# The first weight piece's products token tile by token tile, two norms on ScalarE, and weights rounded in units of two pieces

## The chip, the cores and the metric

The kernel runs on one core of one Trainium2 chip. The metric is the device time of one execution in microseconds; the time of a kernel is the median of its runs. Before the change it is 1092.45 us, the median of 9 runs from 1089.96 to 1096.31. A profiled execution gives the start and duration of every instruction on each engine: TensorE (PE in the profile; its weight loads PEld), VectorE (DVE), ScalarE (ACT), GpSimd (POOL) and the queue of SyncE that issues transfers (SPq).

## The reference

`x` comes from an attention in chunks of 64 tokens (8 batches, 8 heads, 576 tokens, head size 64), with heads side by side, so that it is 8 x 576 x 512. Then:

```python
X = np.fft.fft(x, axis=1)
X = np.fft.fft(X, axis=2)
u = x + np.real(X).astype(np.float32)
mu = np.mean(u, axis=-1, keepdims=True)
var = np.mean((u - mu) ** 2, axis=-1, keepdims=True)
un = (u - mu) / np.sqrt(var + 1e-06)
out = u + np.maximum(un @ w_ch1, 0.0) @ w_ch2      # w_ch1 512 x 2048, w_ch2 2048 x 512
```

The weights are given in double precision; the kernel computes in 32 bits, so it has to round each weight itself.

## The kernel before

**Tokens.** Tokens are taken in tiles of 128. Four tiles of a batch (two "low" and two "high", mirrored ones) make a group; each pair of batches also has a tile of the remaining tokens. Group 0 is batch 0.

**Start.** `attention_early` computes batch 0's attention. `fourier_early` then multiplies by the tables of the transform along the tokens into four sums `z` and a row `mid` (L742, L745), copies them to `zf` and `zr` (L752 to L768), and multiplies by the tables along the features into `early_xp` (L772). For each pair of tiles it adds the result to `x` (L786 to L790), takes mean and variance (`means`, L634 to L639: two instructions on VectorE, then logarithm and exponential on ScalarE), norms the tile (`normed`, L820 to L826), and transposes it on TensorE into `unT` (`turned`, copies on L839). Where TensorE would wait, `keep_warm` gives it products of zeros (L1143).

**The two layers.** `up_first` takes group 0 through the first layer: for each four of the sixteen feature tiles it goes over four weight pieces (kk), with four products of 512 token columns for each, and then ScalarE takes the relus (L940). `down_plain` goes over the sixteen pieces of the second layer (`dn`, L970), four products each. Each such group of four products is one step of the main loop, which counts them in `t`: steps 1 to 16 end in `up_first`, step 17 and on in `down_plain`. After every step the loop draws from a list of side work (attention and Fourier of the next batch, `side`), and then rounds weights: one call of `round_next`, two calls in steps up to 4, at every fourth and from step 19, and none where the side work says it was heavy. Batch 1's side work falls in steps 3 to 25; its last softmax of a tile comes at step 14, folds at 16 and 18, its sums `z` at 22 and 23, its mixes at 24 and 25. From step 23, `conv2` (L897) adds work on VectorE. Group 1's tiles are normed and turned from the tenth piece of `dn` on. Every engine carries out its instructions in the order in which the program names them.

**Rounding.** A weight piece is 128 x 512 doubles, read as pairs of 32-bit words, `lo` and `hi`. There are 32 pieces, 16 for each layer. `round_weight(i)` issues what this text calls the head of piece i and then the tail of piece i - 1. A head is two ANDs on VectorE (L306, L309), each followed by ScalarE: `fraction` (L300), and `exponent` with two instructions (L303, L304). A tail is three instructions on VectorE (L318 to L320), after which the piece can be used. Raw pieces lie in seven spaces, five later on; a piece is loaded (L285, on SP's queue) when a tail has freed a space. The first heads and the first tail are issued at the end of `attention_early`; the ScalarE part of piece 1 is put off until after the first copies of `fourier_early`.

**PSUM.** `ps_f` has four buffers of a bank each (`idle`, `early_xp`, `mid`, later `up` and `dn`), `ps_a` one of two banks (scores, half of `z`), `ps_t` two for transposes and mixes.

Of the kernel before, what the change touches and what calls it, by code (L numbers as in the profile page):

```python
# [16 lines left out]
def kernel(  # L17
# [32 lines left out]
    nc = tc.nc  # L50
# [66 lines left out]
    for b in range(B):  # L117
# [20 lines left out]
    spaces = [yall.rearrange("p a b -> p (a b)")[:, i * 1024:(i + 1) * 1024] for i in range(2)] + [  # L138
        xall[:, r:r + 2, :].rearrange("p a f -> p (a f)")[:, 0:1024]
        for r in (2 * G, 2 * G + 2, NR + 1, G, G + 2)  # L140
    ]
    N_LATE, N_EARLY, N_LAST = 5, 8, 26
# [129 lines left out]
    power = {}  # L272

    raws, free = {}, list(range(len(spaces)))

    def raw(i):
        return spaces[raws[i]].bitcast(U32).rearrange("p (f r) -> p f r", r=2)

    def load_weight(i):

        fit = [r for r in free if (i < N_EARLY or r < N_LATE) and (i < N_LAST or r > 1)]
        if i < len(pieces) and fit:
            raws[i] = fit[0]
            free.remove(fit[0])
            nc.sync.dma_start(out=raw(i).rearrange("p f r -> p (f r)"), in_=pieces[i][1].bitcast(U32))  # L285

    def round_weight(i, later=None):
# [6 lines left out]
        if i < len(pieces):  # L294
            w, t = pieces[i][0], raw(i)
            lo, hi, wi = t[:, :, 0], t[:, :, 1], w.bitcast(U32)
            p = power[i] = three_p.tile([128, 512], U32, tag="o", name="power")
# [4 lines left out]
            def exponent(p=p):  # L302
                nc.scalar.activation(out=p, in_=p, func=ACTF.Relu, scale=-1.0, bias=top[:, 0:1])  # L303
                nc.scalar.activation(out=p, in_=p, func=ACTF.Relu, scale=-8.0, bias=top[:, 1:2])  # L304
# [5 lines left out]
            if later is None:  # L310
                exponent()
            else:
                later += [fraction, exponent]
        if 0 < i <= len(pieces):
            w, t = pieces[i - 1][0], raw(i - 1)
            lo, hi = t[:, :, 0], t[:, :, 1]
            p = power.pop(i - 1)
# [3 lines left out]
            r = raws.pop(i - 1)  # L321
            if i - 1 + len(spaces) < N_EARLY or r < N_LATE:
                free.append(r)
            load_weight(max(raws, default=i - 1) + 1)
# [203 lines left out]
    def attention_early():  # L528
# [32 lines left out]
        keep_warm(6)  # L561
        turn_tables()
        round_next()
        round_next(put_off)

    def attention(b):

# [706 lines left out]
```

## Time and profile before

| | us |
|---|---|
| median of 9 runs | 1092.45 |
| lowest, highest | 1089.96, 1096.31 |
| the profiled execution | 1090.56 |
| its span, first to last instruction | 1088.8 |
| TensorE busy | 1072.3 |
| VectorE busy | 577.2 |
| ScalarE busy | 298.2 |
| GpSimd busy | 280.9 |
| first product of `up_first` | 52.93 |
| first product of `dn` | 121.76 |
| first transposes of group 1 | 174.31 |

A line of the timeline gives the start in us, the time until the last of the merged instructions ends, the engine, the line of the kernel, the operation, what it writes and reads, partitions x elements, how many instructions are merged, and in brackets how long the engine sat idle before and what released it. Durations overlap at their ends, since the next instruction starts before the last has written all it has; so the distance between two starts is what an instruction costs its engine. The granted clock of TensorE is 1.00 in all slices, 0.999 in the mean.

### The profile page before, as it was taken

What the parts mean: (1) busy time and instruction counts of PE and PEld (TensorE: products, weight loads), DVE (VectorE), ACT (ScalarE), POOL (GpSimd) and SP (SyncE); (2) the same over time, 40 slices, a digit from 0 to 9 for tenths busy, and PEclk for the clock granted to TensorE, in tenths of its full rate; (3) what the DMA queues carried; (4) which work ended last, traced back from release to release, by engine and by line L of the source; (5) the groups of instructions that cost most, each with busy time, mean ns of one, the idle gap of its engine ahead of it and who ended that gap; (6) DMA issues with size and microseconds to landing.
All of it is one profiled execution on the core that took longest, in us unless ns stands there. A gap on an engine that the chain in (4) does not pass through costs nothing.

```text
span 1088.8 us, 18830 instructions
## 1 busy us (share of the span) xinstructions
PE 1072.3 (98%) x7016; PEld 849.5 (78%) x7016; DVE 577.2 (53%) x1260; ACT 298.2 (27%) x725; POOL 280.9 (26%) x403
## 2 busy tenths in 40 slices
PE   8999999999999999999999999999999999999998
PEld 6644454446888888888888888888888888888887
DVE  4798987314567355663556455735663534323411
ACT  4687563222113310322022212321133103101300
POOL 4300102444405240254024220514051401210140
PEclk9999999999999999999999999999999999999999
DMA  8767656679575647692668357764653355446232
GB/s 173 228 183 194 157 164 227 178 240 297 188 204 177 191 136 208 193 254 98 199 176 255 117 165 224 202 171 153 197 185 90 146 195 159 122 152 211 78 116 78
DMA packets 147971, 192.73 MB, mean 177 GB/s; under 512 B 66127, under 2 KB 104015, under 8 KB 140713
## 3 DMA queue, kind: packets, MB, share of 16 engines
q1 hardware_dynamic: 145620, 190.20, 58.3%
q8 instruction: 56, 0.92, 0.3%
q0 software_dynamic: 512, 0.68, 0.3%
q10 hardware_dynamic: 1748, 0.66, 0.3%
q14 instruction: 35, 0.28, 0.1%
HBM read 167.22 MB, written 24.12 MB: 176 GB/s over the span
## 4 chain that ended last, share of the span: by engine, by line
PE 88%; DMA 3%; DVE 3%; SPq 2%; ACT 2%; issue 1%; DVEq 0%; ACTq 0%
PE pb L1065 20%; PE pa L1016 17%; PE pa L1065 15%; PE pb L1016 13%; PE dn L970 5%; PE up L949 4%; PE pt L330 3%; PE up L932 2%; PE more_z L649 2%; PE mix L697 2%; PE z L649 2%; PE xp L429 2%; PE sc L381 1%; DMA xall<-in_moe_w_ch_dram 1%; SPq L195 1%; DMA k<-in_k_dram 1%
## 5 line engine op out<-in xcount | busy, mean ns | idle before, releaser
L1016 PE MATMUL pa<-unT,wa 128*128 128x256 f32 x672 | 159.4, 380 | 0.1
L1016 PEld LDWEIGHTS pa<-unT,wa 128*128 128x128 f32 x672 | 126.6, 190 | 17.7 <-DVE wa L1024 0.5
L922 POOL TENSOR_TENSOR h<-h 128x256 f32<-128x256 f32 x64 | 56.0, 881 | 268.8 <-PE pb L1016 150.5
L1065 PE MATMUL pa<-wb,h 128*128 128x256 f32 x512 | 115.6, 380 | 0.0
L1065 PE MATMUL pb<-wb,h 128*128 128x256 f32 x512 | 114.9, 379 | 0.0
L1065 PEld LDWEIGHTS pa<-wb,h 128*128 128x128 f32 x512 | 96.1, 190 | 13.4 <-issue 0.5
L1016 PE MATMUL pb<-wa 128*128 128x256 f32 x448 | 106.6, 381 | 0.0
L1065 PEld LDWEIGHTS pb<-wb,h 128*128 128x128 f32 x512 | 96.3, 190 | 12.6
L1016 PEld LDWEIGHTS pb<-wa 128*128 128x128 f32 x448 | 84.3, 190 | 11.5
L932 PE MATMUL up<-unT,wa 128*128 128x512 f32 x128 | 58.0, 600 | 2.0 <-ACT h L940 1.2
L970 PE MATMUL dn<-wb,h 128*128 128x512 f32 x128 | 57.4, 596 | 1.3 <-ACT h L940 1.3
L1065 PE MATMUL pb<-wb,yall 128*128 128x256 f32 x256 | 58.2, 381 | 0.0
L1022 DVE TENSOR_TENSOR wa<-pb,wa 128x256 f32<-128x256 f32 x56 | 23.5, 423 | 65.4 <-ACT wa L1021 65.4
L1065 PE MATMUL pa<-wb,yall 128*128 128x256 f32 x256 | 57.9, 380 | 0.0
L1065 PE MATMUL pb<-wb 128*128 128x256 f32 x256 | 57.7, 379 | 0.0
L949 PE MATMUL up<-unT,wa 128*128 128x512 f32 x128 | 56.8, 595 | 0.0
L1021 ACT COPY wa<-pa 128x256 f32<-128x256 f32 x56 | 20.9, 373 | 124.7 <-PE pa L1016 124.7
L1016 PE MATMUL pa<-wa 128*128 128x256 f32 x224 | 53.5, 382 | 0.0
L1016 PE MATMUL pb<-unT,wa 128*128 128x256 f32 x224 | 52.9, 379 | 0.0
L1065 PEld LDWEIGHTS pa<-wb,yall 128*128 128x128 f32 x256 | 47.7, 190 | 6.4
L714 POOL TENSOR_TENSOR xall<-y,xall 128x513 f32<-128x513 f32 x14 | 21.3, 1519 | 121.7 <-DVE y L708 121.7
L1065 PEld LDWEIGHTS pb<-wb,yall 128*128 128x128 f32 x256 | 47.7, 190 | 6.3
(242 smaller groups left out, 1676.2 us busy)
## 6 DMA issues: line engine op xcount, KB each, us to landing
wb<-s SPq DMA_DIRECT2D x56, 1024.0 KB
wa<-s SPq DMA_DIRECT2D x196, 256.0 KB
xall<-in_moe_w_ch_dram SPq DMA_DIRECT2D x22, 512.0 KB
q<-in_q_dram SPq DMA_DIRECT2D x96, 112.0 KB
k<-in_k_dram SPq DMA_DIRECT2D x96, 112.0 KB
v<-in_v_dram SPq DMA_DIRECT2D x124, 64.0 KB
yall<-in_moe_w_ch_dram SPq DMA_DIRECT2D x10, 512.0 KB
s<-wb SPq DMA_DIRECT2D x20, 256.0 KB
```

The lines of the kernel that those rows point to most:

```text
L330: nc.tensor.transpose(pt[:, j, :], src(j), ident)
L429: nc.tensor.matmul(out=xp[0][e][t0:t0 + CH, j * DV:(j + 1) * DV], lhsT=a[r0:r0 + CH, j, t0:t0 + CH], rhs=b[r0:r0 + CH, c, j, :], start=Tru ...
L649: nc.tensor.matmul(out=out_, lhsT=lhsT[p], rhs=tk[p, i, T // 2 if T != 5 else 0, cols], start=start, stop=stop, skip_group_check=True,)
L697: nc.tensor.matmul(out=mix[:, cols], lhsT=zt[:, T], rhs=tab, start=(T == 0), stop=(T == 3), skip_group_check=True,)
L714: eng.tensor_tensor(out=x[:, 0:w], in0=y[:, 0:w], in1=x[:, 0:w], op=ALU.add)
L922: nc.gpsimd.tensor_tensor(out=h1[:, m, hi], in0=h1[:, m, lo], in1=h1[:, m, hi], op=ALU.subtract)
L932: nc.tensor.matmul(out=up, lhsT=w1[:, kk, m * 128:(m + 1) * 128], rhs=unT[:, kk], start=(kk == 0), stop=(kk == KD - 1),)
L949: nc.tensor.matmul(out=up, lhsT=w1[:, kk, m * 128:(m + 1) * 128], rhs=unT[:, kk], start=(kk == 0), stop=(kk == KD - 1),)
L970: nc.tensor.matmul(out=dn, lhsT=h1[:, m, s * 128:(s + 1) * 128], rhs=w2[:, m, :], start=(m == 0), stop=(m == KF - 1),)
L1016: nc.tensor.matmul(out=dst, lhsT=w[:, kk, r], rhs=rhs[o][:, kk], start=(o in (0, 1) and kk == 0), stop=(kk == 1), skip_group_check=True,)
L1022: nc.vector.tensor_tensor(out=b, in0=pbs[r][:, 0], in1=a, op=ALU.add)
L1065: nc.tensor.matmul(out=dst, lhsT=lhs[:, m], rhs=w[:, m], start=(o in (0, 2) and m == 0), stop=(m == HF - 1), skip_group_check=True,)
```

## The change

1. **Products by token tile.** The first step of `up_first` (weight piece 0, four feature tiles) is taken out of it. `fourier_early` now has a function `columns(s)`, which multiplies one turned token tile (128 columns) by piece 0 for four feature tiles. Tiles 0 and 1 are multiplied as soon as they are turned, tiles 2 and 3 at the end. The four sums lie in `first_ups`: two buffers of `ps_f` and the two banks of `ps_a`. The relus of the two sums in `ps_a` are issued after all four products.
2. **Norms.** Tiles 0 and 1 of group 0 are normed on ScalarE, with their shift; tiles 2 and 3 stay on VectorE. Statistics, norms and turns have a new order. Of the `keep_warm` in `fourier_early` three go between the products of `z`, one of four after `early_xp`, and of the two before each turn one in all is left.
3. **Rounding.** The 32 pieces form 22 units of one or two pieces: (0), (1), (2,3), (4,5), (6), then (7,8), (9,10), (11) and so on in fives, and the last five alone. Every instruction of a unit works on the whole unit. A unit of two has its power in a part of `w2` that isn't filled yet. A unit is loaded after the tail of the unit that held its space (`last_in`). `round_next` counts its calls and goes on when there are as many as the next unit has pieces; two calls a step are made until step 1 instead of 4. `need(i)` issues the rounding of a piece that the next products use, where it isn't issued yet.
4. **Order at the start.** Piece 0's tail follows its own head at once; piece 1's head is issued after the `zf` copies, two thirds of its ScalarE part before the first statistics and the last (`power_`) after the two norms on ScalarE; its tail comes with the main loop's first call that goes on.

```diff
+    units = [((0,), both_y[:, 0:1]), ((1,), both_y[:, 1:2]), ((2, 3), third), ((4, 5), second), ((6,), single)]
+    last_in = [None] * 5
+    for i in range(7, 26, 5):
+        units += [((i, i + 1), both_y), ((i + 2, i + 3), third), ((i + 4,), single)]
+        last_in += [len(last_in) - 3 if i > 7 else 1, len(last_in) - 2 if i > 7 else 2, len(last_in) - 1 if i > 7 else 4]
+    units += [((27,), both_y[:, 0:1]), ((28,), both_y[:, 1:2]), ((29,), third[:, 0:1]), ((30,), third[:, 1:2]), ((31,), single)]
...
+    def rounded(u):
+
+        i, n = units[u][0][0], len(units[u][0])
+        if i >= KF:
+            return w2[:, i - KF:i - KF + n, :]
+        at_ = [j % KD * (DFF // 512) + j // KD for j in units[u][0]]
+        if n == 1:
+            return in_wa[:, at_[0]:at_[0] + 1]
+        step = at_[1] - at_[0]
+        return in_wa[:, at_[0]:at_[1] + 1:step] if step > 0 else in_wa[:, at_[0]:at_[1] - 1 if at_[1] else None:step]
...
-        round_next()
-        round_next(put_off)
+        round_weight(0)
+        round_weight(1, parts="t")
...
-            if i == order[0]:
-                keep_warm(3)
...
+        round_weight(1, put_off, "h")
...
-        keep_warm(4)
+        idle[0] = mid
+        for do in put_off[:2]:
+            do()
+        keep_warm(3)
         yield
...
+        ups = ps_a.tile([128, 2, 512], FP32, tag="att", name="up_a")
+        first_ups.extend([ps_f.tile([128, 512], FP32, tag="ff", name="up") for _ in range(2)])
+        first_ups.extend([ups[:, i] for i in range(2)])
+
+        def columns(s):
+
+            for m, up in enumerate(first_ups):
+                nc.tensor.matmul(
+                    out=up[:, s * 128:(s + 1) * 128], lhsT=w1[:, 0, m * 128:(m + 1) * 128],
+                    rhs=unTs[0][:, 0, s * 128:(s + 1) * 128], start=(s == 0), stop=False, skip_group_check=True,
+                )
...
-            if i > 0:
+            if i == 0:
+                normed(0, 0)
+            if i == 1:
+                turned(0, 1)
+                columns(0)
+            means([high])
+            if i == 0:
                 normed(0, 1)
-                turned_(1)
-            normed(0, 2 * i)
-            means([high])
-            turned_(2 * i)
+                turned(0, 0)
+                keep_warm(1)
+        put_off[2]()
+        columns(1)
+        normed(0, 2)
+        turned(0, 2)
         normed(0, 3)
-        turned_(3)
+        turned(0, 3)
+        columns(2)
+        columns(3)
...
+            ups = first_ups if f == 0 else [ps_f.tile([128, G * 128], FP32, tag="ff", name="up") for _ in range(4)]
             for kk in range(KD):
-                for m, up in enumerate(ups, f):
+                need(f + kk)
+                for m, up in enumerate(ups, f) if f + kk > 0 else ():
...
         def round_next(later=None):
+            nonlocal n_w, owed
+            owed += 1
+            if n_w <= len(units) and (n_w == len(units) or owed >= len(units[n_w][0])):
+                owed -= len(units[n_w][0]) if n_w < len(units) else 0
+                round_weight(n_w, later)
+                n_w += 1
...
-                    if t <= 4 or t < KF and t % 4 == 0 or t >= KF + 3:
+                    if t <= 1 or t < KF and t % 4 == 0 or t >= KF + 3:
                         round_next()
```

## The prediction

> **What bounds the kernel now.** I read the page first, then the waits of TensorE, then its order of time in the first 70 us, then VectorE and ScalarE over the same stretch.
>
> ```profile
> PE 1072.3 (98%) x7016; PEld 849.5 (78%) x7016; DVE 577.2 (53%) x1260; ACT 298.2 (27%) x725; POOL 280.9 (26%) x403
> ```
>
> TensorE is busy for 98% of the span. After 122 us its waits are under 1 us each, so a stall taken out early should shorten the run, unless another engine has less in hand than TensorE's early start asks for. In the busy time stand 64 records of `keep_warm` (19.8 us), which compute nothing.
>
> ```profile
> 31.57 1.21 PE L742 MATMUL z<-tk,pm 128*128 128x289 f32 x4 [0.34 <-POOL pm_rest L523]
> 33.92 1.73 PE L1143 MATMUL idle<-warm 128*128 128x289 f32 x6
> 40.63 3.44 PE L772 MATMUL early_xp<-start,zf 128*128 128x256 f32 x14 [0.73 <-DVE zf L752]
> 43.90 3.08 PE L1143 MATMUL idle<-warm 128*128 128x289 f32 x12
> 52.93 10.57 PE L932 MATMUL up<-unT,wa 128*128 128x512 f32 x24 [0.68 <-ACT unT L839]
> 69.60 0.70 PE L932 MATMUL up<-unT,wa 128*128 128x512 f32 x1 [1.17 <-ACT h L940]
> ```
>
> Timeline of TensorE. From 41 to 52.93 us it waits for four normed tiles. Then `up` runs; a product has two records of 0.43 us, so a step of four products is 3.44 us. The next stall is at 69.60, for the relus.
>
> ```profile
> 37.15 0.49 DVE L306 TENSOR_SCALAR wa<-yall 128x512 uint32<-128x512 uint32 x1 [3.53 <-DMA yall<-in_moe_w_ch_dram]
> 40.16 0.42 DVE L752 COPY zf<-z 128x256 f32<-128x256 f32 x1
> 42.29 0.69 DVE L786 TENSOR_TENSOR xall<-early_xp,xall 128x512 f32<-128x512 f32 x1 [0.65 <-PE early_xp L772]
> 112.99 0.68 DVE L394 TENSOR_REDUCE mx<-sc 128x8 f32<-128x512 f32 x1
> 162.81 0.42 DVE L707 TENSOR_TENSOR y<-y,mix 128x255 f32<-128x255 f32 x1 [0.86 <-ACT y L703]
> ```
>
> VectorE. The wait for piece 1 at 37.15 holds up the rounding of piece 0 and behind it the `zf` copies. The last two lines matter most: at 112.99 it takes up the softmax without a wait, 0.95 us after the scores started, and at 162.81 it has only 0.86 us in hand. Between them it works nearly without a gap.
>
> ```profile
> 119.22 0.63 ACT L300 ACTIVATE wb<-wb 128x512 f32<-128x512 uint32 x1 [2.27 <-DVE wb L306]
> 121.13 2.04 ACT L940 ACTIVATE h<-up 128x512 f32<-128x512 f32 x4
> 121.76 3.70 PE L970 MATMUL dn<-wb,h 128*128 128x512 f32 x8 [1.34 <-ACT h L940]
> 153.18 0.72 ACT L304 ACTIVATE power<-power,top 128x512 uint32<-128x512 uint32 x1
> 153.81 0.35 ACT L675 COPY zf<-z 128x256 f32<-128x256 f32 x1
> ```
>
> ScalarE's queue. The relus, and later the `zf` copies of batch 1, stand behind the rounding of whatever piece VectorE has just begun. A late VectorE reaches TensorE this way.
>
> **The change, step by step.** Unmarked times are on the clock of the trace; "new" marks mine.
>
> *Fourier products.* Three `keep_warm` between the products of `z` go: 33.92 to 35.48, so 1.56 us earlier. The rest of piece 0's rounding no longer stands behind piece 1's head: it follows ScalarE's last step (ends 35.31) and leaves VectorE free at new 36.7, before `z` is ready. So the 0.73 us stall goes, and the first add moves from 42.29 to new 39.7. Piece 1's head (0.68 us) now fits ahead of it, with the piece landed at 37.15. ScalarE does two of piece 1's three steps before the first logarithm, which moves from 44.45 to new 41.4.
>
> *Norms.* On ScalarE a norm takes 0.33 from logarithm to exponential, 0.66 over both shifts to `un`, and 0.72 until the next instruction (171.16, 171.49, 171.60, 171.82, 172.15, 172.87). Two such chains from 41.4 end at 44.8; then, in queue order, copy of tile 0 (0.49), logarithm and exponential (0.44), copy of tile 1, the same pair for tile 3, the put-off third step of piece 1 (0.65), which ends at new 47.4. Tiles 2 and 3 are normed on VectorE (0.47 each, the latter after its exponential, at 46.8) and copied by 48.5 and 49.0.
>
> *Products by token tile.* Sixteen products of 128 columns, 32 records; a record of 129 columns starts 0.11 us after its neighbour (156.45 to 156.68 for two), so 0.9 us a tile, 3.5 us in all against 3.44 for the step removed. Two tiles fall in gaps; the last ends at new 50.4. Step kk=1, formerly at 56.37, can start 5.9 us earlier.
>
> *Rounding in units.* A single head takes 0.68 us (L306 53.59 to L318 54.27), a single tail 1.92. A 128x256 TENSOR_TENSOR took 0.42 and a 128x512 0.69, so 512 more elements add 0.53: each tail instruction goes from 0.60 to 1.13, with the 0.12 bubble 3.51 for a pair against 3.84. A 1024-wide AND is not in the trace: at the rate of the single (0.34) it adds 0.27, head 1.20; at the rate of the others 0.53 more, head 2.27. No row of it runs faster than 0.34, so 1.20 is the lower end. I take 1.20, the same instruction's rate. [...]
>
> From new 47.3 VectorE does head (2,3), then the tail of piece 1, ready at 50.5: no stall. Head (4,5) and tail (2,3) follow: 50.4 + 1.20 + 3.51 and the write, 55.2. But kk=2 wants them at 53.9: a new stall of 1.3 us. Before, piece 2 was ready at 56.28 for 59.81. Lead now 4.6.
>
> *The borrowed PSUM.* Two of the first four sums lie in the tile that the scores need, so the scores wait for all four relus, not the next products for the first. ScalarE: copies of q and k, rounding of piece 6 (1.9), relus (2.04): new 64.2. Scores 0.65, next products at new 64.95 against 69.60. The old wait of 1.17 us is taken over by this one. **Lead 4.65.**
>
> *What is late next: VectorE's backlog.* Calls are cut (two a step until step 1, not 4) and a pair waits for two calls. When the scores of step 4 come, six pieces are done instead of eight, and VectorE waits 5 us for them. Going on through the calls, it also idles about 3 us at step 7, 2 at 11 and 4 before step 14, its last softmax of batch 1, which starts at 112.04 - 4.65 + 0.76 = new 108.15. By then 17 tails and 19 heads are done; before, 21 and 22. So four tails and three heads remain, 4 x 1.92 + 3 x 0.68 = 9.7 us, less about 1.7 for pairs. These are due by the same steps 15 to 23. In order:
>
> - Softmax 1.33, head (19,20) 1.20, tail (17,18) 3.51, two transposes 1.87, first AND of 21: 116.5. ScalarE's three steps 1.9, relu and latency 0.65: `dn` starts at new 119.05, against 121.76. Lead 2.7; the wait there grows from 1.34 to over 3.
> - Head 21 and tail (19,20) 4.2, attention and folds 6.34 (121.36 to 127.70): 126.6; then batch 1's last tile, 127.05 to 131.0 (3.93). Tail 21 and head (22,23) 134.1, steps 20 to 22 until head 30 at 151.2. ScalarE's three steps, then 2.9 of `zf`/`zr` copies: 156.05. TensorE wants these from 153.7 on; mix ends at new 156.3 against 157.55. Lead 1.2.
> - Tails 29 to 31 until 157.9, three L897 2.0, y 2.47, two L897 1.2: the next y at new 163.6, against 162.81, with 0.86 in hand used up. From y to the normed first tile of group 1 the trace takes 10.15 (162.81 to 172.96), so its transposes start at 173.9 against 174.31. **Lead 0.4.**
>
> *Queues.* SP issues the same 32 loads; a pair is loaded after its predecessor's whole tail. A load takes 3.6 us from issue to use (136.25 to 139.87), a second in its shadow some 6. Only pair (14,15) is 0.6 us late, inside an idle stretch. Once that cover is gone the 0.6 is lost. POOL's queue is passed by nothing. Wider instructions on ScalarE (about 0.96, 1.18, 1.07 for a pair) always end before the tail's second instruction.
>
> *Clock.* Granted clock 1.00 in every stretch, also in 51.00 to 54.40 with TensorE busy 2.73 of 3.40; in the new order its longest gap is some 0.7 us, so nothing is charged. [...]
>
> **Sum.** -5.9 at kk=1, +1.3 at the pair, -0.05 at the relus, +1.95 at `dn`, +1.5 at mix, +0.8 at the first transposes of group 1: -0.4 against the profiled 1090.56 us (span 1088.8). That execution is 1.89 below the median of the runs, so 1092.45 - 0.4, rounded to 1092.0. A change under 0.2% (2.2 us) can hardly be told from none.
>
> **Rivals.**
> - *The lead holds* because the backlog is hidden: 1092.45 - 4.65 = 1087.8; with half, 1090. For it: no row shows TensorE waiting for a weight piece, and the margins there are up to 20 us. Against it: 0.86 us in hand at 162.81, and ScalarE's 153.18 to 153.81 without a gap.
> - *Slower: the wide AND at single rate.* Five heads count (two before pair (2,3), three after step 14), 1.07 each: -0.4 + 5.35 = +4.9, 1097.3. It turns the sign from 0.1 us a head, passes 0.2% from 0.5. For it: the source steps by two and the target by whole blocks, a form no row has.
> - *Slower: a pair's blocks are ordered as one stretch.* Pair (4,5) lies on both sides of piece 1; if its head waits for kk=1 to end (53.9), kk=2 starts 3.5 us later, and pairs (7,8) and (14,15) stall likewise for 3 and 4.3: about +9 to +10, 1102. Against: no row shows such a wait; before, every piece is one block.
> - *The step is not earlier at all*, if ScalarE's two norms take as long as VectorE's: then -1.5 of the front stays and 4.25 is given back: +2.7, 1095.
>
> **How the numbers follow.** Main case 0.46, all within 0.2%, its own range 1090.3 to 1094.2 (an error of 1 us in the front and 1.5 in the backlog). Lead held in good part 0.26. Single rate 0.12, one stretch 0.07, front not earlier 0.09: 0.28 slower. The range runs from 1087.5 (lead held) to 1097.5 (single rate) and leaves the one-stretch case out.
>
> **What would show it.** First `up` record of 128 columns about 45.5, kk=1 about 50.5; L306 of 1024 elements 0.6 to 0.7 us; TensorE waiting over 1 us before the third step and for relus before the scores; a wait of 3 us or more before `dn`; VectorE idle around 60 to 65 and 104 to 108. Wrong if TensorE waits at neither `dn` nor mix, or if L306 takes 1.1.

## The result

The changed kernel takes 1098.18 us (median of 10 runs, 1095.46 to 1100.50) against 1092.21 for the kernel before (32 runs): a ratio of 1.0054, 95% interval 1.0042 to 1.0066. It is 5.9 us slower. 1092.0 was predicted, with a range from 1087.5 to 1097.5. The profiled execution took 1098.45 us, its span is 1096.7.

TensorE's timeline after the change. Times are starts; in brackets the idle time ahead and what ended it.

```profile
33.28 1.21 PE L766 MATMUL z<-tk,pm 128*128 128x289 f32 x4 [1.78 <-POOL pm_rest L549]
...
47.29 0.69 PE L811 MATMUL up<-unT,wa 128*128 128x128 f32 x4
...
52.33 1.96 PE L975 MATMUL up<-unT,wa 128*128 128x512 f32 x4
...
57.05 1.98 PE L975 MATMUL up<-unT,wa 128*128 128x512 f32 x4 [1.04 <-DVE wa L345]
...
66.28 0.69 PE L405 MATMUL sc<-kT,qT 64*64 64x64 f32 x32 [1.22 <-issue]
66.91 1.55 PE L975 MATMUL up<-unT,wa 128*128 128x512 f32 x3
...
121.01 3.70 PE L1019 MATMUL dn<-wb,h 128*128 128x512 f32 x8 [3.28 <-ACT h L984]
...
156.13 0.49 PE L721 MATMUL mix<-ce,zr 128*128 128x129 f32 x2 [0.26 <-ACT zr L702]
...
157.89 0.70 PE L721 MATMUL mix<-cx,zr 128*128 128x256 f32 x2 [0.83 <-ACT zr L709]
...
158.81 3.60 PE L1019 MATMUL dn<-wb,h 128*128 128x512 f32 x8
...
164.62 0.46 PE L721 MATMUL mix<-ce,zf 128*128 128x129 f32 x2 [1.11 <-DVE y L732]
...
177.44 0.66 PE L354 MATMUL pt<-ident,un 128*128 128x128 f32 x4 [0.36 <-ACT un L864]
...
216.94 0.70 PE L405 MATMUL sc<-kT,qT 64*64 64x64 f32 x32 [1.37 <-DVE rd L466]
...
233.34 0.69 PE L405 MATMUL sc<-kT,qT 64*64 64x64 f32 x32 [0.70 <-DVE rd L466]
```

The front does what it was to do: step kk=1 starts at 52.33, formerly 56.37, although `z` starts 1.71 us later here. In the profiles of this study `z` starts between 31.57 and 35.30 us, and that of the kernel before is the earliest. In both profiles it starts 0.10 us after the last copy of its table `tk` on ScalarE (these end at 31.47 and 33.18), and the first of these copies starts at 29.35 and 31.06, once the table's transfer has landed. The change moves nothing ahead of that transfer, so I take the difference as chance, which no run tests. "Lead" below is the kernel before's time from the start of `z` less the changed kernel's:

| TensorE at | before | after | lead | predicted |
|---|---|---|---|---|
| kk=1 | 56.37 | 52.33 | 5.75 | 5.9 |
| kk=2 | 59.81 | 57.05 | 4.47 | 4.6 |
| after the first relus | 69.60 | 66.91 | 4.40 | 4.65 |
| first `dn` | 121.76 | 121.01 | 2.46 | 2.7 |
| `dn` after the first mix | 157.55 | 158.81 | 0.45 | 1.2 |
| first transposes of group 1 | 174.31 | 177.44 | -1.42 | 0.4 |
| scores with the fifth k that VectorE transposes | 228.31 | 233.34 | -3.32 | 0.4 |
| end of the span | 1088.8 | 1096.7 | -6.19 | 0.4 |

Down to `dn` every step came within 0.25 us. Then the lead is lost faster than I had worked out, and after 177 us, where I charged nothing, another 4.8 us go.

VectorE's timeline after the change:

```profile
49.05 0.69 DVE L330 TENSOR_SCALAR wa<-xall 128x1024 uint32<-128x1024 uint32 x1
49.65 0.68 DVE L333 TENSOR_SCALAR wb<-xall 128x1024 uint32<-128x1024 uint32 x1
...
53.38 1.22 DVE L343 SCALAR_TENSOR_TENSOR wa<-xall,wa 128x1024 f32<-128x1024 uint32 x1
...
67.03 0.69 DVE L418 TENSOR_REDUCE mx<-sc 128x8 f32<-128x512 f32 x1 [5.84 <-PE sc L405]
...
110.10 0.69 DVE L418 TENSOR_REDUCE mx<-sc 128x8 f32<-128x512 f32 x1 [3.51 <-PE sc L405]
...
215.80 1.08 DVE L373 STREAM_TRANSPOSE kT<-k 128x512 f32<-128x512 f32 x1 [8.60 <-DMA k<-in_k_dram]
...
232.19 1.09 DVE L373 STREAM_TRANSPOSE kT<-k 128x512 f32<-128x512 f32 x1 [5.86 <-DMA k<-in_k_dram]
```

A wide AND costs 0.60 us (49.05 to 49.65), and a pair's head 1.20 as predicted. Before its four softmaxes VectorE idles 14.6 us in all (1.7 before), so the last tail ends at 161.75 (156.06 before; of the 5.7 us between them 1.7 are the later start of `z`). The last two lines are transposes of k, for which VectorE waits. It waits for the same two tiles in the kernel before; these are VectorE's transposes and TensorE's scores there:

```profile
210.49 1.10 DVE L349 STREAM_TRANSPOSE kT<-k 128x512 f32<-128x512 f32 x1 [6.46 <-DMA k<-in_k_dram]
...
227.14 1.12 DVE L349 STREAM_TRANSPOSE kT<-k 128x512 f32<-128x512 f32 x1 [6.21 <-DMA k<-in_k_dram]
```

```profile
212.21 0.65 PE L381 MATMUL sc<-kT,qT 64*64 64x64 f32 x32
...
228.31 0.69 PE L381 MATMUL sc<-kT,qT 64*64 64x64 f32 x32 [0.46 <-DVE rd L442]
```

There the first k is early enough for the scores, and the second is 0.46 us late. In the changed kernel the scores wait 1.37 and 0.70 us behind the two.

The order on ScalarE ahead of `dn`:

```profile
118.47 0.63 ACT L322 ACTIVATE wb<-wb 128x512 f32<-128x512 uint32 x1 [3.04 <-DVE wb L330]
119.01 0.71 ACT L325 ACTIVATE power<-power,top 128x512 uint32<-128x512 uint32 x1
119.75 0.72 ACT L328 ACTIVATE power<-power,top 128x512 uint32<-128x512 uint32 x1
120.38 2.04 ACT L984 ACTIVATE h<-up 128x512 f32<-128x512 f32 x4
```

The relus wait behind piece 21's three steps, which wait 3.04 us for VectorE to begin the piece.

### The profile page after: what moved, and what is told of

Same layout as the page of the kernel before. It is cut to its first block, busy times and chain, and to the rows that moved or that the text cites. A ratio compares the mean times of both kernels' runs of the same rounds, so it can differ in the third digit from the quotient of the medians.

```text
span 1096.7 us, 18762 instructions
## 1 busy us (share of the span) xinstructions
PE 1070.2 (98%) x7018; PEld 847.6 (77%) x7018; DVE 572.1 (52%) x1208; ACT 292.8 (27%) x700; POOL 281.9 (26%) x403
## 4 chain that ended last, share of the span: by engine, by line
PE 84%; DVE 5%; DMA 3%; SPq 2%; ACT 2%; issue 1%; POOL 1%; DVEq 0%; POOLq 0%; ACTq 0%
PE pb L1114 20%; PE pa L1065 16%; PE pa L1114 15%; PE pb L1065 13%; PE pt L354 3%; PE up L996 3%; PE up L975 2%; PE dn L1019 2%; PE more_z L673 2%; SPq L204 2%; PE sc L405 2%; PE mix L721 2%; PE xp L453 1%; PE z L673 1%; DMA k<-in_k_dram 1%
## 5 line engine op out<-in xcount | busy, mean ns | idle before, releaser
L1065 PEld LDWEIGHTS pa<-unT,wa 128*128 128x128 f32 x672 | 126.5, 190 | 18.0 <-DVE wb L960 0.6
L996 PE MATMUL up<-unT,wa 128*128 128x512 f32 x128 | 56.8, 596 | 0.0
L1114 PEld LDWEIGHTS pb<-wb 128*128 128x128 f32 x256 | 47.6, 190 | 5.9
```

The costliest lines, as they stand in the source:

```text
L996: nc.tensor.matmul(out=up, lhsT=w1[:, kk, m * 128:(m + 1) * 128], rhs=unT[:, kk], start=(kk == 0), stop=(kk == KD - 1),)
L1065: nc.tensor.matmul(out=dst, lhsT=w[:, kk, r], rhs=rhs[o][:, kk], start=(o in (0, 1) and kk == 0), stop=(kk == 1), skip_group_check=True,)
L1114: nc.tensor.matmul(out=dst, lhsT=lhs[:, m], rhs=w[:, m], start=(o in (0, 2) and m == 0), stop=(m == HF - 1), skip_group_check=True,)
```

## The experiments

Differences are against the kernel before in the same set of runs, in per cent with the 95% interval; 0.1% is 1.1 us. Where a text below gives us, they are these per cents of the kernel before.

| kernel | difference |
|---|---|
| changed | +0.54 (0.42 to 0.66) |
| changed, two calls until step 4 | +0.32 (0.17 to 0.47) |
| before, two calls until step 1 | +0.13 (0.00 to 0.27) |
| changed, single pieces, calls until step 4 | +0.04 (-0.05 to 0.14) |
| changed, single pieces | -0.04 (-0.12 to 0.05) |
| changed, four calls of step 4 ahead of its softmax | +0.18 (0.08 to 0.29) |
| changed, one call owed | +0.24 (0.11 to 0.36) |
| changed, idle products ahead of `dn` | +0.37 (0.24 to 0.51) |
| one call owed, last piece behind the copies | -0.05 (-0.15 to 0.04) |
| the same, step 4's calls ahead | +0.06 (-0.03 to 0.15) |
| single pieces, step 4's calls ahead | -0.16 (-0.26 to -0.07) |
| changed, two k loads on ScalarE | +0.79 (0.62 to 0.96) |
| changed, the next two k loads on ScalarE | +0.64 (0.45 to 0.82) |
| changed, a k load ahead of the output stores | +0.47 (0.34 to 0.61) |
| single pieces, step 4's calls ahead, that k load too | +0.02 (-0.10 to 0.15) |
| one call owed, last piece behind, that k load too | +0.01 (-0.14 to 0.16) |
| single pieces, step 4's calls ahead, conv2 by fours | -0.12 (-0.24 to 0.01) |

**Which part: calls, units or front.** Four runs undo them one by one. The first gives the old calls back:

```diff
-                    if t <= 1 or t < KF and t % 4 == 0 or t >= KF + 3:
+                    if t <= 4 or t < KF and t % 4 == 0 or t >= KF + 3:
```

> The changed kernel with one number back: two rounding calls a step until step 4 (t <= 4), not until step 1. Units of two, products by token tile and the norms stay. Theory A (VectorE's backlog from the fewer calls): the three extra calls fill the 5.84 us that VectorE idles before the softmax at 67.03, so some 7 us of rounding less is left after step 14; the wait for the relus before dn falls from 3.28 to under 2 us, those at mix, y and the transposes of group 1 shrink below 1 us together, and the stalls at 217 and 233 us go with them. Time 1088 to 1091. Theory B (the units themselves, by their size or by loading two at once, make the pieces late): the waits stay within 1 us of the changed kernel's and the time stays at 1095 to 1099. If only part of the loss is the calls, 1092 to 1095.

Measured +3.5 us: about 2.4 of the 5.9 come back. The wait before `dn` is 2.9 us, so by the waits this is theory B; its time, 1097.14, lies in that theory's range. (The edit adds two calls, not three: step 4 has two in any case.) The second makes the opposite edit in the kernel before.

> The kernel before with the same number changed alone: two rounding calls a step until step 1, not until step 4. Nothing else is touched, pieces are rounded singly. Theory A: three pieces (2.6 us each) are pushed behind the softmax of step 14, and without the front's lead of 4.4 us to spend, the run loses what the changed kernel lost from its relus on, 10.6 us, less that lead, and a little more since singles cost more: 1097 to 1100, with the wait before dn up from 1.34 to over 4 us and a wait at the mix. Theory B: the margins of up to 20 us by which pieces were early take it up: within 1 us of the kernel before, 1091.5 to 1093.5.

Measured +1.4 us (0.0 to 2.9), nearer to theory B, with waits of 1.1 for `y` and 0.8 for `zr` at the mix; the wait before `dn` stays at 1.3. Fewer calls alone are cheap. The third keeps the front and goes back to single pieces:

```diff
+    ring = [both_y[:, 0:1], both_y[:, 1:2], third[:, 0:1], third[:, 1:2], single]
+    units = [((0,), ring[0]), ((1,), ring[1]), ((2,), ring[2]), ((3,), ring[3])]
+    units += [((4,), second[:, 0:1]), ((5,), second[:, 1:2]), ((6,), single)]
+    last_in = [None] * 7
+    for i in range(7, 32):
+        units.append(((i,), ring[(i - 7) % 5]))
+        last_in.append((0, 1, 2, 3, 6)[i - 7] if i < 12 else i - 5)
...
-                    if t <= 1 or ...
+                    if t <= 4 or ...
```

> The changed kernel with pieces rounded singly in the same buffers, and two calls a step until step 4 as before: what stays of the change is the products by token tile with their PSUM, the two norms on ScalarE and the order of the first pieces. Theory A: the front's 4.4 us at the first relus stay; VectorE has the work of the kernel before to do by dates that lie 4.4 us earlier, with 0.95 us in hand at the last softmax of step 14 and 0.86 at y, so a part is given back: 1088.5 to 1091, and no stall of 1.04 at the third step. Theory B (the units are what is late): the same 1088 to 1091, but then better than the run with units and t <= 4 by 3 us or more. A third view, that the front brings nothing that reaches the end, gives 1092 or more.

Measured +0.4 us (-0.5 to +1.5): the third view, no gain. TensorE's timeline in that run:

```profile
61.05 1.88 PE L974 MATMUL up_a<-unT,wa 128*128 128x512 f32 x4
...
68.41 1.14 PE L404 MATMUL sc<-kT,qT 64*64 64x64 f32 x32 [5.49 <-issue]
```

and ScalarE's:

```profile
64.37 0.63 ACT L321 ACTIVATE wa<-wa 128x512 f32<-128x512 uint32 x1 [0.35 <-DVE wa L329]
64.91 0.71 ACT L324 ACTIVATE power<-power,top 128x512 uint32<-128x512 uint32 x1
65.65 0.72 ACT L327 ACTIVATE power<-power,top 128x512 uint32<-128x512 uint32 x1
66.28 1.06 ACT L983 ACTIVATE h<-up 128x512 f32<-128x512 f32 x2
```

With the old calls, piece 8 is begun ahead of the first relus, and nearly the whole front is lost in one wait of 5.49 us at the scores. The granted clock behind it is 0.55 from 68 to 70 us and 0.60 from 70 to 72, and at `dn` the lead is 0.08. So the fewer calls let the lead pass the relus, as the next run shows. It has the new calls and single pieces.

> The changed kernel with its own calls (two a step until step 1), but pieces rounded singly in the same buffers: only the units are undone. The first set gave, against the kernel before: fewer calls alone +1.2 us, front with singles and the old calls +0.5, front with units and the old calls +3.5, all together +5.9. If the units with their wait for two calls are the main loss, this run is within +0 to +2 us of the kernel before, 4 to 6 better than the changed kernel, with the scores of step 4 early (waiting under 1.5 us), a wait before dn under 2 us and the k load of the third tile after the first on VectorE's transposes issued before 206. If the fewer calls cost most once the front asks for the pieces earlier, it is +3 to +5.

Measured -0.4 us (-1.3 to +0.5), with the scores of step 4 waiting 1.22 and `dn` 1.37. Undoing the units alone takes the whole loss back. The units are its cause, within the order that the change gives them. A unit is three things at once: wider instructions, loads of two pieces, and a start that waits for two calls.

**Why units lose, when a pair's tail is cheaper than two.** Two runs keep the units. One lets a pair go at the first of its two calls, and so every unit one call earlier:

```diff
-        owed = 0
+        owed = 1
```

> The changed kernel with the count of owed calls beginning at one: a unit of two is rounded at the first of its two calls, not at the second; the number of calls is the same. If the wait for the second call is what leaves VectorE idle (14.6 us before four softmaxes against 1.7 in the kernel before), that idle time falls by 3 us or more, the last tail ends 2 to 4 us earlier and the time is 1.5 to 4 us under the changed kernel's (+2 to +4.5 against before). If the idle time comes only from the number of calls, it is within 1 us of the changed kernel, +5 to +7.

Measured +2.6 us, 3.3 under the changed kernel. VectorE's waits from 45 to 170 us (total, times, longest), first the changed kernel's:

```profile
DVE mx L418 <- PE sc L405: 14.6, 4, 5.8
```

and this run's:

```profile
DVE mx L418 <- PE sc L405: 5.8, 1, 5.8
DVE rd L475 <- PE xp L453: 5.6, 2, 3.1
```

The idle time before the softmaxes falls to 5.8 us, and counted from the start of `z` the last tail ends 5.3 us earlier than in the changed kernel. TensorE does not wait at `dn` at all and is there at 116.61, a lead of 6.1. Nothing is computed differently, and the instructions are as wide as before; units are begun one call earlier. It then loses the lead at the mix (below). The other run fills VectorE's idle time at step 4, with the same two more calls as the run with `t <= 4`, in another place:

```diff
+                if t == 4:
+                    for _ in range(4):
+                        round_next()
                 heavy = False
...
-                if not heavy:
+                if not heavy and t != 4:
```

> The changed kernel with its units and its two calls a step until step 1, plus the two calls that the run with t <= 4 added, but placed elsewhere: in step 4 four calls stand ahead of the step's scores and softmax, behind the relus of the first four tiles, and none behind. Theory (VectorE's idle time before the softmaxes is what is repaid later, and rounding put ahead of the relus only moves the wait to the scores): the scores of step 4 wait no more than 1.5 us (2.46 with t <= 4), VectorE's 5.84 us before that softmax are filled, its last tail ends 3 to 5 us earlier than in the changed kernel, the waits at dn, mix and y fall from 5.5 us together to under 3, and the time is 2 to 4 us under the changed kernel's, +2 to +4 us against before. Rival (the loss comes from the units' waits, wherever the calls stand): +4.5 us or more against before.

Measured +2.0 us; the scores of step 4 wait 1.22, and `dn` and mix wait 2.9 us together. The last tail ends at 158.90, which is 2.9 us earlier, but counted from the start of `z` only 1.3, where 3 to 5 were expected. The run with `t <= 4` has +3.5 with as many calls, so the place is worth about 1.5 us; the two intervals overlap. Part of it is the clock: four of these twelve executions have a mean clock of 0.998 or less, and nine of the twelve with `t <= 4`.

**The clock.** TensorE's granted clock after the wait at `dn`: rows of the view by stretches (columns: stretch, its length, TensorE's busy time, its weight loads, VectorE, ScalarE, GpSimd, then granted clock, DMA share, GB/s). First the changed kernel's profile:

```profile
118.50:122.50 4.00, 1.49 (x4) 0.78 (x5) 3.93 (x6) 3.88 (x7) 0.00 (x0) 1.00 1.09 261
```

then the second of the runs with k loads on ScalarE (below), which also waited 3.28 us there:

```profile
118.50:122.50 4.00, 2.67 (x3) 1.17 (x4) 3.61 (x7) 2.71 (x6) 0.22 (x2) 0.50 1.08 217
122.50:126.50 4.00, 4.00 (x10) 1.87 (x9) 3.40 (x11) 0.00 (x0) 0.00 (x0) 0.64 1.06 304
```

The first eight `dn` records took 3.70 us in the one and 6.42 in the other. The run that fills the wait with work on zeros:

```diff
+        if g == 0:
+            idle[0] = ps_t.tile([128, 512], FP32, tag="pt", name="idle")
+            keep_warm(5)
         for m in range(KF):
```

> The changed kernel with five products of zeros on TensorE ahead of the first dn products, in the 3.28 us in which it waits there for the relus; nothing else. In the traces so far the granted clock stands at 0.5 for one or two stretches of 3.41 us after such waits (after 117 us in the runs with t <= 4, with the four calls ahead and in both with k loads on ScalarE; at the mix in the run with one call owed), and of the changed kernel's eleven runs eight show a mean clock of 0.998 or less, of the kernel before none in the last set. Theory: a wait of 2 to 5 us halves the clock for the next 3.41 us or twice that, 1.7 or 3.4 us of work lost each time, which is about a third of the changed kernel's loss. Then here nearly all runs show 0.999 or more and the time is 1.2 to 2.5 us under the changed kernel's: +3.4 to +4.7 us against before. Rival (the lower clock comes from elsewhere, or costs nothing that reaches the end): unchanged, +5.4 or more.

Measured +4.0 us, 1.9 under the changed kernel; five of its six executions have a mean clock of 0.999 or more, of the changed kernel's eleven only three. Its `dn` starts with the changed kernel's lead (2.44), so little but the clock has moved. The changed kernel's own executions agree: those three took 1095.46, 1095.48 and 1098.45 us, the eight with a lower clock 1096.65 to 1100.50. So on the median about a third of the loss goes with a lower clock, and products in a wait that I had predicted take it away; the intervals of the two kernels overlap, so the size is rough. The changed kernel's own profile shows none of it: it caught the slowest of the three executions without. Eight profiles of other kernels show a lower granted clock, down to 0.50, behind a wait, for some 3.4 or 6.8 us by my estimate (last section).

A lower clock hits the run with one call owed too, at the mix (0.53, 0.50, 0.50 and 0.76 in the four stretches of 2 us from 154 to 162); TensorE's timeline there (all eleven of its executions have a mean clock of 0.998 or less):

```profile
154.09 0.80 PE L721 MATMUL mix<-ce,zr 128*128 128x129 f32 x2 [2.62 <-ACT zr L702]
...
155.85 1.23 PE L721 MATMUL mix<-cx,zr 128*128 128x256 f32 x2 [0.51 <-ACT zr L709]
...
157.29 5.42 PE L1019 MATMUL dn<-wb,h 128*128 128x512 f32 x8
```

There the last piece's three steps stand ahead of the `zf` and `zr` copies on ScalarE. One call fewer in step 22 puts them behind:

```diff
-                    if t <= 1 or t < KF and t % 4 == 0 or t >= KF + 3:
+                    if t <= 1 or t < KF and t % 4 == 0 or t >= KF + 3 and t != KF + 6:
```

> The run with one call owed, and the second call of step 22 left out, so that the head of the last piece comes after the zf and zr copies of batch 1, as in the changed kernel. In the run with one call owed TensorE was early at dn (by 5 us on the kernel before) and lost it at the mix: 2.62 and 0.51 us of waiting for zr behind the last piece's three steps on ScalarE, and then 6.8 us at half clock, in every one of its runs (mean clock 0.997). Theory: with the copies ahead of that piece the wait falls under 1 us, the clock stays at 1.00, and the time falls by 3 to 5 us: -2.5 to -0.5 us against before. If the lead is lost at the next place instead (y, the transposes of group 1, k): -0.5 to +1.5.

Measured -0.5 us (-1.6 to +0.4), on the edge between theory and rival: `dn` (115.94) and the mix (151.51) are reached early, and the lead is lost between the mix and the k loads. Ten of its eleven executions have a mean clock of 0.999 or more. With one number and one call moved, the changed kernel, units and all, is level with the kernel before. So the loss came from when the units begin, not from their width. Filling step 4's idle time there, and in the run with single pieces:

```diff
+                if t == 4:
+                    for _ in range(2):
+                        round_next()
                 heavy = False
...
-                if not heavy:
+                if not heavy and t != 4:
```

> The kernel of the previous entry with the two calls of step 4 ahead of that step's scores and softmax, in VectorE's 5.8 us of idle time there. Theory: VectorE's last tail ends another 2 to 3 us earlier, and as long as y and the transposes of group 1 are what limits, the time falls by 0.5 to 2 us against the previous entry: -4 to -1 us against before. If VectorE is no longer what limits, no difference beyond 0.5 us.

> The changed kernel with pieces rounded singly and its own calls (it came out level with the kernel before), with the two calls of step 4 ahead of that step's scores and softmax. In that run VectorE idled 4.7 us before three softmaxes, 3.5 of them at step 4, and TensorE waited 1.1 at y and 1.9 for k. Theory: the idle time at step 4 is filled, VectorE's last tail ends 3 us or more earlier, the waits at y and for k go, and the time is -3.5 to -1.5 us against before. If the front's lead is lost elsewhere: -1 to +1.

The first is +0.7 us (-0.3 to +1.6): nothing gained. The second, -1.7 us (-2.8 to -0.8; medians 1090.56 and 1092.42), is faster than both kernels, the only faster one here whose interval excludes no change. It is the best of seventeen kernels and was not measured again as it stands, so part of the -1.7 may be the choice. It too reaches `dn` 5.8 us ahead by the lead above, and keeps under a third of that.

**Where leads end: SP's queue.** In every profile in which SP issues it behind the output stores, the k load for the scores at 217 comes 20.8 to 22.8 us after conv2's last difference starts on VectorE (before: 180.50 and 201.64; after: 184.92 and 207.01). Ahead of it stand conv2's stores, the next q and six output stores. The first attempt to move it moved the wrong loads:

```diff
-        for src, dst, nm, eng in ((q, qs, "q", nc.sync), (k, ks, "k", nc.scalar if n == 0 else nc.sync)):
+        for src, dst, nm, eng in ((q, qs, "q", nc.sync), (k, ks, "k", nc.scalar if n == 0 or n - first[2] in (1, 2) else nc.sync)):
```

> The changed kernel with the k loads of the second and third tile of batch 2 issued from ScalarE's queue instead of SP's, all else equal. Theory A's second half: SP's queue from 176 to 217 us is conv2's stores, the loads and the output stores one behind the other, so VectorE's late conv2 makes the k loads late and TensorE stalls 1.37 us at 217 and 0.70 at 233. From ScalarE's queue k lands early: both stalls fall below 0.5 us, time 1096 to 1097. Rival (the DMA engines themselves were slow in that one profiled run, or k is late for another reason): the stalls in the profile do not change, time 1097.5 to 1099.

Measured +8.6 us: not 1 us better but 2.7 worse. These k tiles aren't the late ones, and the first of the loads waits in ScalarE's queue ahead of the relus; the wait before `dn` grew to 4.93 us, and the granted clock is 0.62 from 118 to 122 us and 0.53 from 122 to 126. The second attempt has (3, 4) in place of (1, 2): the fourth and fifth k that VectorE transposes.

> The changed kernel with two k loads of batch 2 issued from ScalarE's queue, this time those of the fourth and fifth tile that VectorE transposes, which are the ones that TensorE waited for (transposes at 215.80 and 232.19 in the changed kernel; the first attempt moved the loads of the two tiles before them). Theory: SP's queue, 22 us from conv2's last difference to this k load, is what makes k late; from ScalarE's queue it is issued some 8 us earlier, the stalls of 1.37 and 0.70 us vanish, and the time is 1.5 to 2.5 us under the changed kernel's, +3.5 to +4.5 us against before. Rival (k is late because the DMA engines are busy, whichever queue issues it): both stalls stay above half of their size, +5 us or more.

Both stalls are gone (scores at 216.91 and 232.64 without a wait), as the theory has it, but the time is +7.0 us, the rival's. The loads hold ScalarE up for 2.48 and 7.66 us, and a slab of weights came 3.3 us late in that profile. So what the two stalls cost can't be read from this time. The clean test exchanges two entries of SP's queue:

```diff
-                    store(n, o)
+                    if g == 0:
+                        kept.append((n, o))
+                    else:
+                        store(n, o)
...
+                if t == 2 * KF + 1:
+                    for n, o in kept:
+                        store(n, o)
```

> The changed kernel with one exchange in SP's queue: the k load of the fourth tile that VectorE transposes (207.01) goes ahead of the six output stores of group 0 (199.47 to 206.9). Theory (SP's queue makes k late): the load is issued at 199 to 200, its transpose falls from 215.80 to 209 or less, the stall of 1.37 us at the scores of 217 goes, and the time is 1 to 2 us under the changed kernel's: +4 to +5 us against before. Rival (transfers are slow whatever their order, or something later takes it back): the transpose comes no earlier than 213, or the time stays at +5.4 or more.

VectorE's timeline in this run, its transposes of k:

```profile
206.92 1.10 DVE L373 STREAM_TRANSPOSE kT<-k 128x512 f32<-128x512 f32 x1
...
232.05 1.08 DVE L373 STREAM_TRANSPOSE kT<-k 128x512 f32<-128x512 f32 x1 [6.28 <-DMA k<-in_k_dram]
```

and TensorE's, the scores:

```profile
215.25 0.65 PE L405 MATMUL sc<-kT,qT 64*64 64x64 f32 x32
...
233.18 0.69 PE L405 MATMUL sc<-kT,qT 64*64 64x64 f32 x32 [2.29 <-DVE rd L466]
```

The first k is 9 us earlier and its stall gone; the second is where it was, and its wait grows from 0.70 to 2.29. Together 2.29 against 2.07: nothing gained there. The time, +5.1 us, lies on the edge between theory and rival. The same exchange in the two mended kernels:

> The best kernel so far (singles, the two calls of step 4 ahead of its softmax; -1.9 us against before) with the same exchange on SP. TensorE's lead of some 4 us at 160 is gone by 240, with waits of 2.5 us for VectorE's rd behind the late k and 1.4 for kT. Theory: the 1.0 us at 211 goes and the later ones shrink, -2.5 to -4 us against before. Rival: the lead is lost at the next load instead, -1.2 to -2.4.

> The changed kernel with the three small mends together: one call owed at the start, the last piece's head behind the zf and zr copies, and the exchange on SP; units of two, products by token tile and the norms on ScalarE stay as changed. Without the exchange it was -0.5 us against before. Theory: -1.5 to -3. Rival, as in the entry before: -1 to 0.

+0.2 and +0.1 us: neither gains, and the first is worse than even its rival's case. Six of its twelve executions have a mean clock of 0.998 or less; its profile is not one of them, so where that clock is lost stays open. In its profile too the first stall is gone, and the fifth k's is 2.32 us. The profile of the second started late (`z` at 35.30) and says little.

What the exchange leaves is the fifth k load, which stands on SP behind everything from conv2's end on. In every profile in which SP issues it, that is 41.2 to 44.0 us after conv2's last difference starts: 180.50 and 222.26 before, 184.92 and 227.50 after, 184.46 and 226.62 in the kernel before with fewer calls, 179.32 and 221.93 in the fastest. Six kernels reach the first transposes of group 1 with a lead of 1.8 to 3.4 us; at the scores with the fifth k 0.1 to 1.4 of it is left. The fixed distance alone does not prove that conv2 is the reason: in every run so far conv2's last difference starts 6.2 or 7.5 us after TensorE's first transposes of group 1, so the load keeps much the same distance to these too. The last run parts the two and moves conv2's end:

```diff
                 if n_w > len(units) and t >= KF + 7:
-                    for _ in range(3):
+                    for _ in range(4):
```

> The best kernel (singles, the two calls of step 4 ahead of its softmax) with conv2 drawn four times a step instead of three; nothing else. Theory (SP's queue from conv2's stores to the fifth k load is the limit at 227): conv2's last difference falls from 179.32 to 176 or 177, the fifth k load is issued 2 to 3 us earlier (219 to 220 instead of 221.93), TensorE's waits there shrink, and the time is -2.8 to -4.5 us against before. Rival (the stores of the last pieces land no earlier, or the scores of batch 2 are now behind conv2 on VectorE): the load is not earlier by more than 1 us, or the time stays at -1 to -2.4 or rises.

Measured -1.3 us (-2.6 to +0.1). Conv2's last difference starts at 176.68 and the load is issued at 219.77, both as expected, though 0.9 us of each is an earlier `z`. Counted from `z`, the first transposes of group 1 come 1.5 us later than in the best kernel and the load 1.3 us earlier, so the load follows conv2. The scores there wait no more: the lead is 1.95 at the transposes and 2.41 at the scores. But the time is no better than the best kernel's, since of TensorE's waits (total, times, longest) these have grown:

```profile
PE pt L353 <- ACT un L863: 2.0, 3, 1.1
...
PE mix L720 <- DVE y L731: 1.7, 1, 1.7
```

VectorE does conv2 ahead of `y` and the means now, and is late there. The wait has moved back to VectorE, the engine that the change tried to relieve.

## Why the prediction was wrong

- **Right:** kk=1 (5.75 for 5.9), the new stall for pair (2,3) (1.04 for 1.3), the scores behind all four relus (4.40 of lead for 4.65), a pair's head and tail (1.21 and 3.53 for 1.20 and 3.51), VectorE's idle time (5, 3, 2 and 4 us predicted; 5.84, 3.14, 2.06 and 3.51 measured), and a wait of more than 3 us at `dn` (3.28). In the rows 512 more elements cost the AND 0.26 us (0.34 to 0.60), about what its own rate gave (0.27), not the 0.53 of the TENSOR_TENSORs. So three rivals are out: the wide AND at single rate (the 0.53), the pair's blocks as one stretch (the head of pair (4,5) starts at 52.18, ahead of kk=1, and kk=2 waits 1.04 us, not 3.5 more), the front not earlier. Down to `dn` the mechanism of the main case is the one that ran.
- **Mis-sized: +1.5 at mix and +0.8 at the first transposes of group 1.** They took 2.0 (2.46 to 0.45) and 1.9 (0.45 to -1.42), 1.6 us more together. The mix waited twice for `zr`, 0.26 and 0.83, where I had counted its start alone, and 1.11 for `y`, whose delay I had priced only at the transposes. That delay was also larger: VectorE's list has the last tail end at 157.9, and on the same clock it ended at 160.0. Of these 2.1 us, 1.2 are two waits (0.52 and 0.67) for ScalarE's steps of the last piece, which stood behind the `zf` and `zr` copies.
- **The step that failed: the sum ends at the first transposes of group 1.** I ended VectorE's list there, though conv2 and its stores on SP stood in the code, and costed "Queues" by the weight loads alone. The lead of 0.4 us that I ended with was to hold to the end; the profile loses 4.8 us behind that point, 1.9 of it up to the fifth k. That VectorE's lateness reaches k by conv2 and SP is shown by the run that moved a k load in the queue (its transpose 8.9 us earlier, its stall gone) and by the one that moved conv2's end. That mending it would win the time back is not shown, since the next waits took it. Of the other 2.9 us some are at slabs and operands of the later groups (0.20, 0.72 and 0.53), and a k at 586.55 waits 1.47 (0.73 before). Profiles of other kernels have between none and 1.8 us at the slabs, and 3.3 in one; how much is chance stays open.
- **The step that failed beside it: "Clock ... nothing is charged".** I weighed gaps in the front alone, and predicted a gap of 3 us at `dn` two paragraphs earlier. The run with idle products puts it at 1.9 us on the median, though the profiled execution shows none.
- **The rival that I held for second likeliest, the lead holds,** was refuted as stated. Its ground, margins of up to 20 us at the weight pieces, was true and beside the point: TensorE never waited for a piece after kk=2. It waited for relus, copies and k, which stand behind the pieces in in-order queues.

I also took the profiled 1090.56 as a typical execution less 1.89 us. The profile that I started from was one with an early `z`; the median difference, 5.9, is smaller than that of the two profiles, 7.9. The changed kernel's profile, in turn, is 3.0 us slower than its two other executions with nearly full clock, so some of what it loses is its own, the 1.7 us at `z` among it. As an estimate on the median, the sum was short by 6.3 us (-0.4 for +5.9): 1.6 from the two mis-sized terms, 1.9 up to the fifth k and 1.9 of clock make 5.4, and the rest is open.

## What to carry to other kernels

An engine's lead is worth what the busiest in-order queue behind it leaves over: follow the late engine's every product to its last consumer, stores and the loads queued behind them included, before the sum is closed. Wider units save instructions and time (a pair's head and tail took 4.74 us here, two single ones 5.20) but come due as a whole; if a counter paces them, let a unit begin at its first call, and put the calls where the engine idles and no relu or copy stands behind them. And a predicted wait on TensorE is to be priced with the clock that can follow it: here one of 2.04 us was followed by some 3.4 us at 0.50, one of 3.28 in one profile by 6.8, in another by none (next section).

## What was not expected of the hardware

The length of a wait on TensorE does not tell here whether a lower clock follows. The granted clock by the view by stretches, behind such waits:

| kernel | wait, us | granted clock, from:to in us |
|---|---|---|
| changed, two calls until step 4 | 2.86 at `dn` | 0.53 in 124:126, 0.61 in 126:128 |
| changed, single pieces, calls until step 4 | 5.49 at the scores of step 4 | 0.55 in 68:70, 0.60 in 70:72 |
| changed, single pieces | 2.99 at `z` | 0.83 in 30:40 |
| changed, four calls of step 4 ahead of its softmax | 2.04 at `dn` | 0.62, 0.50, 0.50, 0.67 in the four us of 121:125 |
| changed, one call owed | 2.62 and 0.51 at the mix | 0.53, 0.50, 0.50, 0.76 in steps of 2 us in 154:162 |
| one call owed, last piece behind the copies | 0.70 and 0.82 at the mix | 0.66, 0.50, 0.50, 0.64 in the four us of 153:157 |
| changed, two k loads on ScalarE | 4.93 at `dn` | 0.62 in 118:122, 0.53 in 122:126 |
| changed, the next two k loads on ScalarE | 3.28 at `dn` | 0.63, 0.50, 0.50, 0.66 in steps of 2 us in 118:126 |
| changed | 3.28 at `dn` | 1.00 in 118.5:126.5 |
| changed, idle products ahead of `dn` | 0.67 at `dn` | 1.00 in 118.5:126.5 |

Four of the rows go down to 0.50. If the lower clock is 0.50 in the others too, then as an estimate from these rows (what a stretch lacks to 1.00, times its length, over 0.5) it held for about 3.4 us in five of the eight profiles and for about 6.8 in three; behind the wait of 2.04, for instance, for 0.76 + 1 + 1 + 0.66 us. A wait of 3.28 us was followed by it in one profile and not in the other. Two waits of 0.70 and 0.82 were (TensorE was busy 0.49 and 0.44 us in the two us from 151 to 153), in the only one of that kernel's eleven executions with a mean clock of 0.998. So no bound comes out.
